# Seven products per tile summed by PSUM in two banks, and six more such tiles, in a spectral mixer with a squared-ReLU layer pair

## The chip, the cores and the metric

One core of one Trainium2 chip runs the whole program. The metric is the device time of one execution in microseconds (us). Before the change it is 845.22 us, the median of three runs (844.39 to 845.75). The engines are called PE (matrix products; PEld is its loading of weights), DVE or VectorE, ACT or ScalarE, POOL or GpSimd, and SP, which issues most transfers.

## What is computed

Eight sequences of 3008 rows and 256 columns go through a mixer in the frequency domain, and the 24064 rows that come out go through two layers:

```python
X = np.fft.rfft(x, axis=1)                       # x: (8, 3008, 256)
Yr = Xr @ w_r - Xi @ w_i + b_r
Yi = Xr @ w_i + Xi @ w_r + b_i
Y  = shrink(Yr, 0.01) + 1j * shrink(Yi, 0.01)    # sign(v) * max(|v| - 0.01, 0)
y  = np.fft.irfft(Y, n=3008, axis=1).reshape(24064, 256)

h = y @ w_in                                     # (24064, 2048)
g = s * np.maximum(h, 0) ** 2 + b
out = g @ w_out                                  # (24064, 256), float32
```

`s` and `b` are single numbers, so `out` is `s * (r*r @ w_out)` plus a row that is the same everywhere (`bias_bc` in the kernel: `b` times the column sums of `w_out`).

## The kernel before, in words

**Tiles.** The rows are cut into 48 tiles of mostly 512 rows (T0 to T47; a few have 480 or 384). T0 to T11 belong to the first two sequences, which the code calls batches. Batches 2 to 7 begin at T12, T17, T23, T29, T35 and T41. For each tile PE makes the first layer in 16 slots: in a slot, the two `psh` matmuls of 512 columns give 128 of the 2048 features (`first_mm`, L847). After every second slot ScalarE rectifies two such blocks (L867: `rt <- psh`), and ScalarE (L877) or VectorE (L880) squares them into `gt`, as 16-bit numbers with the features in partitions. A running account of each engine's load (`work`, `act_first`) chooses which of the two. The second layer of tile T runs one tile later, spread over the 16 slots of T + 1's first layer. Into the same slots go the units of the Fourier stages of other batches (`plan`): the `psf` matmuls, the `ring`, `xf`, `u`, `v` and `yt` operations.

**The plain second layer** (`second_mms`, L918): four groups of 16 matmuls of 256 columns, two groups to a PSUM bank of the pool `psa`; then one VectorE operation on each bank (L941) multiplies by `s`, adds the bias row and gives the output rows, which SP stores. That is 64 matmuls of 256 columns.

**The second layer by seven products** (`seven_mms`, L979). The squares of a tile are seen as two by two blocks a11, a12, a21, a22 (half of the rows; even or odd feature block), and so are the weights w11, w12, w21, w22 (even or odd feature block; half of the output columns). Sums of the weights are made once (`make_t`, L369: T0 to T3). Sums of the squares are made for each tile in two parts, q = 0 and 1 (`s_op`, L961), in place except for the first:

- S1: s1 = a21 + a22
- S3: a21 becomes a11 - a21
- S2: a11 becomes a11 - s1
- S4: a12 becomes a12 + the new a11. This one is an adding DMA that POOL issues (L969), the other three are VectorE's (L976).

The seven products, each of 16 matmuls of 128 columns (two groups of 128 rows, eight feature blocks), are in the numbers that the changed code uses: P1 = a11 w11, P2 = a12 w21, P3 = a12' w22, P4 = a22 T3, P5 = s1 T0, P6 = a11' T1, P7 = a21' T2, where a dash marks a block after its sum. The output blocks are P1 + P2 (top left), P1 + P6 + P5 + P3 (top right), P1 + P6 + P7 + P4 (bottom left) and P1 + P6 + P7 + P5 (bottom right), with all signs in the sums.

Before the change the products come in the order P1, P2, P4, P5, P6, P7, P3 (in the code `left[0]` to `left[6]`), each in its own half of a bank, four banks to a tile from a pool of two. `leave` (L1016) sums them on VectorE in SBUF, in a tile `zz`, in four groups: after P1 and P2 (two adds and one operation with `b_21`, L1026), after P4 (one), after P5 and P6 (one, and one of 512 columns for both halves of `zz`), after P7 and P3 (three), then four stores. A bank is taken again by the next pair of products but one: P5 and P6 wait for the adds of P1 and P2.

Of the 48 tiles 22 are made so (`seven`, L1063): T4 to T7, the two before the start of batches 2 to 7 where they have 480 or 512 rows (10, 11, 15, 16, 21, 22, 27, 33, 34, 39), the second tile of batches 3 to 7 (18, 24, 30, 36, 42), and from T41 on all such but the last two (41, 42, 43, 45).

**Order.** A scheduler lays the program out before it runs: each engine has a fixed order of instructions, near to the order of the code, though an instruction that would wait may be placed behind others. An engine carries out its list in order, so a waiting instruction holds all behind it.

Of the kernel before, what the change touches and what calls it, by code (L numbers as in the profile page):

```python
# [10 lines left out]
F32 = mybir.dt.float32  # L11
ALU = mybir.AluOpType
# [84 lines left out]
def kernel(  # L97
# [48 lines left out]
    apool = ctx.enter_context(tc.tile_pool(name="psa", bufs=2, space=bass.MemoryType.PSUM))  # L146
# [66 lines left out]

    def other_bank():
        return apool.tile([P, 512], F32, name="psa", tag="psa")
# [146 lines left out]
    b_21 = cpool.tile([P, P], F32, name="b_21")  # L362
# [6 lines left out]
    def make_t(i):  # L369

        if not T_s:
            nc.vector.tensor_tensor(
                out=b_21, in0=bias_bc[:, P:D], in1=bias_bc[:, 0:P], op=ALU.subtract
            )
            T_s.append(x2pool.tile([P, 4, MC // 2, P], F16, name="T_s", tag="x2"))
# [584 lines left out]

    def s_op(ti, n, q):  # L961
# [6 lines left out]
        if n == 4:  # L968
            nc.gpsimd.dma_start(out=a12, in_=a11, accum_op=ALU.add)  # L969
            return  # L970
# [3 lines left out]
            2: (a11, a11, s1, ALU.subtract),  # L974
        }[n]
# [3 lines left out]
    def seven_mms(ti):  # L979

        tl = tiles[ti]
        size = sub_size(tl)
        hold = {}
        left = [(0, 0), (0, 1), (1, 1), None, (0, 0), (1, 0), (0, 1)]
        firsts = (0, 2, 3, 5)
        T = T_s[0]
        right = [w_block(0, 0), w_block(1, 0), T[:, 3], T[:, 0], T[:, 1], T[:, 2], w_block(1, 1)]

        def mm(n, j, c):

# [16 lines left out]
        def add(out, of, other):  # L1007
            nc.vector.scalar_tensor_tensor(  # L1008
                out=out, in0=of, scalar=s_bc[0:size], in1=other, op0=ALU.mult, op1=ALU.add
# [3 lines left out]
        def wide(t):  # L1013
            return t[0:size, 0:P].unsqueeze(1).to_broadcast([size, 2, P])

        def leave(group):  # L1016
            if group == 0:
                hold["z"] = zpool.tile([P, 2, 2, P], F32, name="zz", tag="zz")
            if group in (0, 3):
                hold["o", group] = opool.tile([P, 2, D], F32, name="ost", tag="ost")  # L1020
            z = hold["z"][0:size]
            top = hold["o", 0][0:size]
            if group == 0:
                add(z[:, 0], hold[0], wide(bias_bc))
# [3 lines left out]
            elif group == 1:  # L1028
                add(z[:, 0], hold[2], z[:, 0])
            elif group == 2:  # L1030
                add(z[:, 1], hold[3], z[:, 1])
                two = hold[4].rearrange("p j e -> p (j e)").unsqueeze(1).to_broadcast([size, 2, D])
                zs = z.rearrange("p h j e -> p h (j e)")
                add(zs, two, zs)
                work("dve", 0.27)
            else:
                for h in range(2):
                    add(hold["o", 3][0:size, :, h * P : (h + 1) * P], hold[5], z[:, h])
                add(top[:, :, P:D], hold[6], z[:, 1])
                for i in range(2):  # L1040
# [124 lines left out]
```

## Time and profile before

| | us |
|---|---|
| median of three runs | 845.22 (844.39 to 845.75) |
| profiled execution: its time | 843.5 |
| profiled execution: its span, first to last instruction | 841.7 |

The granted clock of TensorE is 0.999 over the span. The costliest groups of instructions, with the mean of one:

| line, engine | operation | count | busy us | mean ns |
|---|---|---|---|---|
| L175 PE | `psh <- yt, w_in`, 512 columns (and 480) | 1344 | 396.6 | 378 |
| L175 PE | `psa <- w_out_t, gt`, 256 and 128 columns | 2432 | 305.9 | 252 |
| L175 PE | `psa <- T_s, gt`, 128 columns | 992 | 83.4 | 219 |
| L867 ACT | rectify, `rt <- psh`, 1024 columns | 384 | 387.0 | 1009 |
| L880 DVE | square, `gt <- rt` | 238 | 285.2 | 1203 |
| L877 ACT | square, `gt <- rt` | 146 | 151.7 | 1039 |
| L969 POOL | adding DMA of S4 (issue) | 44 | 39.7 | 902 |
| L976 DVE | each of S1, S2, S3, 1024 columns | 40 | 27.5 | 687 |
| L941 DVE | output of a plain bank, 512 columns | 41 | 30.7 | 748 |
| L1008 DVE | one add of the seven products, `ost`, 256 columns | 76 | 34.5 | 479 |

A matmul's duration in the profile includes its way through the array; the next one starts long before it ends. So how fast PE goes is read from one start to the next, not from the mean of one. The share of idle time of an engine matters only where another engine waits for it.

### The profile page before, as it was taken

What the parts mean: (1) busy time and instruction counts of PE and PEld (TensorE: products, weight loads), DVE (VectorE), ACT (ScalarE), POOL (GpSimd) and SP (SyncE); (2) the same over time, 40 slices, a digit from 0 to 9 for tenths busy, and PEclk for the clock granted to TensorE, in tenths of its full rate; (3) what the DMA queues carried; (4) which work ended last, traced back from release to release, by engine and by line L of the source; (5) the groups of instructions that cost most, each with busy time, mean ns of one, the idle gap of its engine ahead of it and who ended that gap; (6) DMA issues with size and microseconds to landing.
All of it is one profiled execution on the core that took longest, in us unless ns stands there. A gap on an engine that the chain in (4) does not pass through costs nothing.

```text
span 841.7 us, 19681 instructions
## 1 busy us (share of the span) xinstructions
PE 823.0 (98%) x7710; PEld 599.3 (71%) x7710; DVE 718.2 (85%) x1120; ACT 722.1 (86%) x959; POOL 87.7 (10%) x116
## 2 busy tenths in 40 slices
PE   8999999999999999999999999999999999999997
PEld 7857767777677767776677666777667767767765
DVE  5988989998898888888888888788889888879885
ACT  5998988998899988988899888889879898788882
POOL 4550001110010001100010000100001000001000
PEclk9999999999999999999999999999999999999999
DMA  8954587356873478436773458614565253513322
GB/s 199 180 152 102 124 195 193 63 104 151 202 177 66 107 173 215 105 90 143 188 184 70 96 137 206 168 53 108 131 175 142 51 109 99 144 45 76 71 64 62
DMA packets 116959, 107.70 MB, mean 128 GB/s; under 512 B 12806, under 2 KB 100874, under 8 KB 115522
## 3 DMA queue, kind: packets, MB, share of 16 engines
q1 hardware_dynamic: 102498, 80.55, 33.7%
q0 software_dynamic: 14368, 25.89, 19.4%
q8 instruction: 60, 0.98, 0.5%
q14 instruction: 33, 0.27, 0.1%
HBM read 53.52 MB, written 46.66 MB: 119 GB/s over the span
## 4 chain that ended last, share of the span: by engine, by line
PE 70%; DVE 11%; ACT 8%; DMA 6%; issue 3%; SPq 1%; POOL 0%; DVEq 0%; ACTq 0%; POOLq 0%
PE psh L175 29%; PE psa L175 25%; PE psf L175 15%; ACT rt L867 3%; DVE gt L880 2%; DVE gt L976 2%; ACT gt L877 2%; DMA vd<-v 1%; DMA ring<-ring 1%; DMA x<-in_x_dram 1%; DVE ring L699 1%; DMA vs<-vd 1%; PE psm L175 1%; DMA gt<-gt 1%; DVE s L976 1%
## 5 line engine op out<-in xcount | busy, mean ns | idle before, releaser
L867 ACT ACTIVATE rt<-psh 128x1024 f32<-128x1024 f32 (+2 forms) x384 | 387.0, 1009 | 66.5 <-PE psh L175 64.3
L175 PEld LDWEIGHTS <-gt 128*128 128x128 f16 (+1 forms) x3728 | 305.1, 101 | 167.7 <-DMA gt<-gt 1.2
L175 PE MATMUL psh<-yt,w_in 128*128 128x512 f16 (+1 forms) x1344 | 396.6, 378 | 0.1
L880 DVE TENSOR_TENSOR gt<-rt 128x1024 f16<-128x1024 f32 (+2 forms) x238 | 285.2, 1203 | 61.1 <-ACT rt L867 59.7
L175 PE MATMUL psa<-w_out_t,gt 128*128 128x256 f16 (+3 forms) x2432 | 305.9, 252 | 1.0 <-DMA gt<-gt 1.0
L877 ACT ACTIVATE gt<-rt 128x1024 f16<-128x1024 f32 (+2 forms) x146 | 151.7, 1039 | 3.5
L175 PEld LDWEIGHTS <-w_in 128*128 128x128 f16 x1536 | 136.2, 98 | 25.3 <-issue 2.6
L175 PE MATMUL psa<-T_s,gt 128*128 128x128 f16 (+1 forms) x992 | 83.4, 219 | 0.0
L969 POOL DMA_DIRECT2D gt<-gt x44 | 39.7, 902 | 379.7 <-DVE s L976 200.3
L699 DVE TENSOR_TENSOR ring<-psf,s 128x512 f16<-128x512 f32 x84 | 57.5, 685 | 3.5 <-PE psf L175 2.7
L187 ACT CAST u<-psf 96x512 f16<-96x512 f32 x91 | 52.6, 580 | 9.1 <-PE psf L175 8.9
L187 ACT CAST v<-psf 128x512 f16<-128x512 f32 x82 | 47.5, 582 | 11.1 <-PE psf L175 11.1
L175 PEld LDWEIGHTS <-xf 128*128 128x128 f16 x504 | 46.5, 98 | 8.7 <-DVE xf L672 1.9
L175 PE MATMUL psh<-tail,w_in 128*128 128x512 f16 (+1 forms) x192 | 52.1, 353 | 0.0
L175 PE MATMUL psf<-W_g,xf 128*128 128x256 f16 x336 | 50.4, 272 | 1.0 <-ACT xf L187 1.0
L234 POOL DMA_DIRECT2D x<-in_x_dram x36 | 19.2, 538 | 265.2 <-PE psf L175 264.1
L187 ACT CAST yt<-psf 128x470 f16<-128x470 f32 (+2 forms) x84 | 43.3, 534 | 4.1 <-PE psf L175 2.9
L1008 DVE SCALAR_TENSOR_TENSOR ost<-psa,s_bc,zz 128x256 f32<-128x256 f32 (+1 forms) x84 | 38.1, 479 | 7.2 <-PE psa L175 6.5
L941 DVE SCALAR_TENSOR_TENSOR ost<-psa,s_bc,bias_bc 128x512 f32<-128x512 f32 (+2 forms) x49 | 35.6, 726 | 6.9 <-PE psa L175 5.0
L175 PE MATMUL psf<-x,A_t 94*96 94x512 f16 x102 | 38.9, 381 | 2.0 <-ACT v L187 0.8
L175 PE MATMUL psf<-C_t,vs 96*128 96x94 f16 (+1 forms) x484 | 37.9, 205 | 0.8 <-DMA vs<-vd 0.8
L187 ACT CAST xf<-psf 128x512 f16<-128x512 f32 x62 | 36.2, 584 | 2.1 <-PE psf L175 1.9
(118 smaller groups left out, 810.7 us busy)
## 6 DMA issues: line engine op xcount, KB each, us to landing
out_dram<-ost SPq DMA_DIRECT2D x152, 128.0 KB
ud<-u SPq DMA_DIRECT2D x56, 192.0 KB
us<-ud SPq DMA_DIRECT2D x28, 384.0 KB
vd<-v SPq DMA_DIRECT2D x42, 256.0 KB
vs<-vd SPq DMA_DIRECT2D x14, 768.0 KB
x<-in_x_dram POOLq DMA_DIRECT2D x28, 376.0 KB, 6.1
gt<-gt POOLq DMA_DIRECT2D x40, 256.0 KB, 4.4
ring<-ring SPq DMA_DIRECT2D x280, 32.0 KB
```

The lines of the kernel that those rows point to most:

```text
L175: return nc.tensor.matmul(out, lhs, rhs, **how)
L187: return None, nc.scalar.copy(out=dst, in_=src)
L234: nc.gpsimd.dma_start(out=t[0:N1, i * w : (i + 1) * w], in_=xv[:, c * XCH * D + i * w : c * XCH * D + (i + 1) * w],)
L699: nc.vector.tensor_tensor(out=ring[0][:, i % 4], in0=ps, in1=hold[i // 2][:, i % 2].unsqueeze(1).to_broadcast([P, 2, D]), op=ALU.add,)
L867: nc.scalar.activation(out=rt[:, :, 0:w], in_=ps[:, :, 0:w], func=AF.Relu)
L877: nc.scalar.activation(out=gt, in_=rr, func=AF.Square)
L880: last_square[0] = nc.vector.tensor_tensor(out=gt, in0=rr, in1=rr, op=ALU.mult)
L941: nc.vector.scalar_tensor_tensor(out=ost[0:size, 0:k], in0=ps[0:size, 0:k], scalar=s_bc[0:size], in1=bias_bc[0:size].unsqueeze(1).to_broad ...
L969: nc.gpsimd.dma_start(out=a12, in_=a11, accum_op=ALU.add)
L976: nc.vector.tensor_tensor(out=out, in0=a, in1=b, op=op)
L1008: nc.vector.scalar_tensor_tensor(out=out, in0=of, scalar=s_bc[0:size], in1=other, op0=ALU.mult, op1=ALU.add)
```

## The change

The order of the products becomes P1, P2, P6, P7, P5, P4, P3, and PSUM does a part of the sums: P6, P5 and P3 are added by PE to what P1 left in one bank (x), P4 to what P7 left in the other (y, which P1's partner P2 used before). VectorE reads a bank between two products of its chain, seven reads to a tile, each right after the product that completes what it reads; the operation with `b_21` and the one of 512 columns are no longer there. Tiles of the last batch use a third bank (w) for P4 and P3 and nine reads.

Six more tiles are made by seven products, the third before the start of each of batches 2 to 7 (T9, T14, T20, T26, T32, T38): 28 in all. In these alone S4 is a VectorE sum. The sums S1 and S3 of part 0 move one slot later (three in the last batch), behind the slot's second-layer matmuls. The two banks of the pool `psa` get a tag each, so that the code says which comes next.

```diff
--- before.py
+++ after.py
@@ -143,7 +143,7 @@
 
     cpool = ctx.enter_context(tc.tile_pool(name="consts", bufs=1))
     bigpool = ctx.enter_context(tc.tile_pool(name="big", bufs=1))
-    apool = ctx.enter_context(tc.tile_pool(name="psa", bufs=2, space=bass.MemoryType.PSUM))
+    apool = ctx.enter_context(tc.tile_pool(name="psa", bufs=1, space=bass.MemoryType.PSUM))
     fpool = ctx.enter_context(tc.tile_pool(name="psf", bufs=2, space=bass.MemoryType.PSUM))
     dpool = ctx.enter_context(tc.tile_pool(name="dram", bufs=2, space=bass.MemoryType.DRAM))
     xpool = ctx.enter_context(tc.tile_pool(name="xp", bufs=3))
@@ -211,8 +211,11 @@
     def sum_bank(ti):
         return any_bank() if ti >= mark[B - 1] // MC else other_bank()
 
+    side = [0]
+
     def other_bank():
-        return apool.tile([P, 512], F32, name="psa", tag="psa")
+        side[0] = 1 - side[0]
+        return apool.tile([P, 512], F32, name="psa", tag=f"psa{side[0]}")
 
 
     XCH = 8
@@ -359,7 +362,6 @@
 
 
     w_sum = small[:, 2:4]
-    b_21 = cpool.tile([P, P], F32, name="b_21")
     T_s = []
     last_square = [None]
 
@@ -369,9 +371,6 @@
     def make_t(i):
 
         if not T_s:
-            nc.vector.tensor_tensor(
-                out=b_21, in0=bias_bc[:, P:D], in1=bias_bc[:, 0:P], op=ALU.subtract
-            )
             T_s.append(x2pool.tile([P, 4, MC // 2, P], F16, name="T_s", tag="x2"))
         t = T_s[0]
         a, b, op = (
@@ -958,6 +957,9 @@
         size = 2 * sub_size(tiles[ti])
         return gts[(ti, q)][:, i, k, :, 0:size]
 
+    def third_last(ti):
+        return any(ti == mark[b] // MC - 3 for b in range(2, B))
+
     def s_op(ti, n, q):
 
         size = 2 * sub_size(tiles[ti])
@@ -965,13 +967,14 @@
             sums[(ti, q)] = spool.tile([P, 4, 2 * P], F16, name="s1", tag="s1")
         s1 = sums[(ti, q)][:, :, 0:size]
         a11, a12, a21, a22 = (part(ti, q, i, k) for i in range(2) for k in range(2))
-        if n == 4:
+        if n == 4 and not third_last(ti):
             nc.gpsimd.dma_start(out=a12, in_=a11, accum_op=ALU.add)
             return
         out, a, b, op = {
             1: (s1, a21, a22, ALU.add),
             3: (a21, a11, a21, ALU.subtract),
             2: (a11, a11, s1, ALU.subtract),
+            4: (a12, a12, a11, ALU.add),
         }[n]
         nc.vector.tensor_tensor(out=out, in0=a, in1=b, op=op)
         work("dve", 0.07 + size / 480.0)
@@ -980,84 +983,99 @@
 
         tl = tiles[ti]
         size = sub_size(tl)
+        alone = ti >= mark[B - 1] // MC
+        C = MC // 2
+        T = T_s[0]
+
+
+        of = {
+            1: ((0, 0), w_block(0, 0), "x"), 2: ((0, 1), w_block(1, 0), "y"),
+            4: ((1, 1), T[:, 3], "w" if alone else "y"), 6: ((0, 0), T[:, 1], "x"),
+            7: ((1, 0), T[:, 2], "y"), 5: (None, T[:, 0], "x"),
+            3: ((0, 1), w_block(1, 1), "w" if alone else "x"),
+        }
+        clears = (1, 2, 4, 7, 3) if alone else (1, 2, 7)
         hold = {}
-        left = [(0, 0), (0, 1), (1, 1), None, (0, 0), (1, 0), (0, 1)]
-        firsts = (0, 2, 3, 5)
-        T = T_s[0]
-        right = [w_block(0, 0), w_block(1, 0), T[:, 3], T[:, 0], T[:, 1], T[:, 2], w_block(1, 1)]
 
         def mm(n, j, c):
 
-            if n in firsts and j == 0 and c == 0:
-                hold["ps"] = sum_bank(ti).rearrange("p (n j e) -> p n j e", n=2, j=2)
-            if j == 0 and c == 0:
-                hold[n] = hold["ps"][0:size, 0 if n in firsts else 1]
+            left, right, to = of[n]
+            if to not in hold:
+                hold[to] = sum_bank(ti).rearrange("p (n j e) -> p n j e", n=2, j=2)[0:size, 0]
+                if to == "y" and not alone:
+                    side[0] = 1 - side[0]
             q, g = divmod(c, 4)
             at = slice(j * size, (j + 1) * size)
-            if left[n] is None:
+            if left is None:
                 lhs = sums[(ti, q)][:, g, at]
             else:
-                lhs = gts[(ti, q)][:, left[n][0], left[n][1], g, at]
+                lhs = gts[(ti, q)][:, left[0], left[1], g, at]
             matmul(
-                hold[n][:, j], lhs, right[n][:, c],
-                start=(n in firsts and j == 0 and c == 0), stop=(c == MC // 2 - 1),
+                hold[to][:, j], lhs, right[:, c],
+                start=(n in clears and j == 0 and c == 0), stop=(c == C - 1),
                 skip_group_check=True,
             )
 
-        def add(out, of, other):
+        def add(out, bank, other):
             nc.vector.scalar_tensor_tensor(
-                out=out, in0=of, scalar=s_bc[0:size], in1=other, op0=ALU.mult, op1=ALU.add
+                out=out, in0=hold[bank], scalar=s_bc[0:size], in1=other, op0=ALU.mult, op1=ALU.add
             )
             work("dve", 0.4)
 
-        def wide(t):
-            return t[0:size, 0:P].unsqueeze(1).to_broadcast([size, 2, P])
-
-        def leave(group):
-            if group == 0:
+        def leave(n):
+
+            if n == 1:
                 hold["z"] = zpool.tile([P, 2, 2, P], F32, name="zz", tag="zz")
-            if group in (0, 3):
-                hold["o", group] = opool.tile([P, 2, D], F32, name="ost", tag="ost")
+            if n in (2, 7):
+                hold["o", n] = opool.tile([P, 2, D], F32, name="ost", tag="ost")
             z = hold["z"][0:size]
-            top = hold["o", 0][0:size]
-            if group == 0:
-                add(z[:, 0], hold[0], wide(bias_bc))
-                add(top[:, :, 0:P], hold[1], z[:, 0])
-                nc.vector.tensor_tensor(out=z[:, 1], in0=z[:, 0], in1=wide(b_21), op=ALU.add)
-                work("dve", 0.34)
...
-        C = MC // 2
-        alone = ti >= mark[B - 1] // MC
+            bias = [
+                bias_bc[0:size, h * P : (h + 1) * P].unsqueeze(1).to_broadcast([size, 2, P])
+                for h in range(2)
+            ]
+            top, bot = (hold["o", k][0:size] if ("o", k) in hold else None for k in (2, 7))
+            if n == 1:
+                add(z[:, 0], "x", bias[0])
+            elif n == 2:
+                add(top[:, :, 0:P], "y", z[:, 0])
+            elif n == 4 and alone:
+                add(z[:, 1], "w", bias[0])
+            elif n == 6:
+                add(z[:, 1], "x", z[:, 1] if alone else bias[0])
+            elif n == 7:
+                add(z[:, 0], "y", bias[1])
+            elif n == 5:
+                add(bot[:, :, P:D], "x", z[:, 0])
+            elif n == 3:
+                add(top[:, :, P:D], "w" if alone else "x", z[:, 1] if alone else bias[1])
+                for j in range(2):
+                    store(tl, j, top[:, j, :])
+            if n == (7 if alone else 4):
+                add(bot[:, :, 0:P], "y", z[:, 1])
+            if n == 5 and alone:
+                add(z[:, 1], "x", bias[1])
+            if n == (5 if alone else 4):
+                for j in range(2):
+                    store(tl, 2 + j, bot[:, j, :])
+
+        turns = [1, 2, 4, 6, 7, 5, 3] if alone else [1, 2, 6, 7, 5, 4, 3]
         early = 3 if alone else 2
         order = [
-            (n, j, c) for h in range(2) for n in range(early) for j in range(2)
+            (n, j, c) for h in range(2) for n in turns[:early] for j in range(2)
             for c in range(4 * h, 4 * h + 4)
         ]
-        order += [(n, j, c) for n in range(early, 6) for j in range(2) for c in range(C)]
-        order += [(6, j, c) for h in range(2) for j in range(2) for c in range(4 * h, 4 * h + 4)]
+        order += [
+            (n, j, c) for n in turns[early:] for h in range(2) for j in range(2)
+            for c in range(4 * h, 4 * h + 4)
+        ]
         slots = [[] for _ in range(MC)]
         for at, what in enumerate(order):
             slots[at // 7].append(lambda w=what: mm(*w))
+            if what[1:] == (1, C - 1):
+                slots[at // 7].append(lambda n=what[0]: leave(n))
         for at, n, q in ((2, 2, 0), (2, 1, 1), (2, 4, 0), (3, 3, 1), (4, 2, 1), (5, 4, 1)):
             at += alone and at > 3
             slots[at].append(lambda n=n, q=q: s_op(ti, n, q))
-        for at, group in ((4 + alone, 0), (6, 1), (11, 2), (15, 3)):
-            slots[at].append(lambda group=group: leave(group))
         return slots
 
     def seven(ti):
@@ -1065,7 +1083,7 @@
             return False
         firsts = [mark[b] // MC for b in range(2, B)]
         return (
-            ti >= firsts[-1] or 4 <= ti < 8 or any(m - 2 <= ti < m for m in firsts)
+            ti >= firsts[-1] or 4 <= ti < 8 or any(m - 3 <= ti < m for m in firsts)
             or any(ti == m + 1 for m in firsts[1:])
         )
 
@@ -1127,10 +1145,12 @@
                 for u in plan.pop(ti * MC + mc, []):
                     u()
                 first_mm(ti, mc)
-                if mc in (10, 11) and seven(ti):
-                    s_op(ti, 1 if mc == 10 else 3, 0)
             for u in nxt[mc]:
                 u()
+            if ti < ti_n and seven(ti):
+                at = 13 if ti > mark[B - 1] // MC else 11
+                if mc in (at, at + 1):
+                    s_op(ti, 1 if mc == at else 3, 0)
     assert not plan
 
 
```

More of the change, by code (lines that the diff above doesn't have):

```diff
@@ L1016, in leave @@
-        def leave(group):
-            if group == 0:
+        def leave(n):
+            if n == 1:
                 hold["z"] = zpool.tile([P, 2, 2, P], F32, name="zz", tag="zz")
-            if group in (0, 3):
-                hold["o", group] = opool.tile([P, 2, D], F32, name="ost", tag="ost")
+            if n in (2, 7):
+                hold["o", n] = opool.tile([P, 2, D], F32, name="ost", tag="ost")
             z = hold["z"][0:size]
-            top = hold["o", 0][0:size]
-            if group == 0:
-                add(z[:, 0], hold[0], wide(bias_bc))
-                add(top[:, :, 0:P], hold[1], z[:, 0])
-                nc.vector.tensor_tensor(out=z[:, 1], in0=z[:, 0], in1=wide(b_21), op=ALU.add)
-                work("dve", 0.34)
[L1028 to L1040, printed above, removed]
-                    for j in range(2):
-                        store(tl, 2 * (1 - i) + j, hold["o", 3 * (1 - i)][:, j, :])
```

## Prediction

> Names: T21 is tile 21; its second layer runs while PE does the first layer of tile 22, slot by slot (16 slots, two psh matmuls each). P1 to P7 are the seven products, sixteen matmuls of 128 columns each; z1, z2, z6 and so on are the VectorE adds that read a bank after the product of that number. S1, S2, S3 and S4 are the sums of squared activations, each made in two parts (part 0, part 1).
>
> **What bounds the kernel now.** First the busy time of each engine, on the page:
>
> ```profile
> PE 823.0 (98%) x7710; PEld 599.3 (71%) x7710; DVE 718.2 (85%) x1120; ACT 722.1 (86%) x959; POOL 87.7 (10%) x116
> ```
>
> PE is the bound, if its 98% is work and not modelled ends. So next who PE waits for (us in total, times, longest):
>
> ```profile
> PE psa L175 <- DVE ost L1008: 2.3, 5, 1.0
> PE psm L175 <- DMA x<-in_x_dram: 2.3, 5, 0.8
> PE psf L175 <- DVE ring L699: 1.8, 5, 0.5
> PE psa L175 <- DMA gt<-gt: 1.0, 1, 1.0
> ```
>
> All lines of that answer add to 12.8 us. Then the pace, from the chain of waits in the window 423 to 433 (start us, us, what), where PE goes from T20's plain second layer to T21's products:
>
> ```profile
> 422.97 0.43 PE psh L175 x2
> 423.40 0.44 PE psa L175 x4
> 423.84 0.43 PE psh L175 x2
> 424.27 0.39 PE psa L175 x7
> 424.66 0.21 PE psf L175 x5
> 424.87 0.43 PE psh L175 x2
> ```
>
> Four plain matmuls of 256 columns take 0.44 us (109 ns each), seven of 128 columns 0.39 (55.6 ns), two of psh 0.43: streaming, with nothing lost between. The reader is to see two things: PE time falls only with columns, and any new wait in PE's order is paid in full.
>
> So the decisive view is VectorE's timeline just where the seven products begin, T21's from 423.68 on, with the two ScalarE rows that its squares wait for (start us, us, operation):
>
> ```profile
> 423.88 0.75 DVE L941 SCALAR_TENSOR_TENSOR ost<-psa,s_bc,bias_bc 128x512 f32<-128x512 f32 x1
> 424.55 1.22 DVE L880 TENSOR_TENSOR gt<-rt 128x1024 f16<-128x1024 f32 x1
> 425.69 0.68 DVE L976 TENSOR_TENSOR gt<-gt,s 128x1024 f16<-128x1024 f16 x1
> 426.29 0.68 DVE L976 TENSOR_TENSOR s<-gt 128x1024 f16<-128x1024 f16 x1
> 426.89 1.22 DVE L880 TENSOR_TENSOR gt<-rt 128x1024 f16<-128x1024 f32 x1
> ...
> 429.19 0.68 DVE L976 TENSOR_TENSOR gt<-gt,s 128x1024 f16<-128x1024 f16 x1
> 429.79 0.48 DVE L1008 SCALAR_TENSOR_TENSOR zz<-psa,s_bc,bias_bc 128x256 f32<-128x256 f32 x1
> 430.30 0.49 DVE L1008 SCALAR_TENSOR_TENSOR ost<-psa,s_bc,zz 128x256 f32<-128x256 f32 x1
> ```
>
> ```profile
> 423.49 1.02 ACT L867 ACTIVATE rt<-psh 128x1024 f32<-128x1024 f32 x1
> 425.41 1.03 ACT L867 ACTIVATE rt<-psh 128x1024 f32<-128x1024 f32 x1
> ```
>
> VectorE runs without a gap here. From start to start a square takes 1.14 us, an S sum 0.60, a following independent add 0.40 (two of them at 442.04 and 442.43, 0.39). The adds of P1 and P2 come only at 429.79, though P1 and P2 were done by 428.6: VectorE is over a microsecond late, and PE pays little, because the bank that these adds free is wanted 16 matmuls later.
>
> **The change, part by part.**
>
> PE columns. Each of the six new tiles trades 64 matmuls of 109 ns (6.98 us) for 112 of 55.6 ns (6.23): 0.75 us, 4.5 us for six. The weight loads double in number against columns but ran hidden in the row of seven above. The Trainium skill, "TensorE: Matmul & The Clock Gate", section "Back-to-back issue gap", speaks against it: a sustained stream of weight loads and 128-column matmuls is said to take about 81 ns each. By it 112 of them would be 9.07 us, 2.1 more than the plain tile, and six tiles an estimated 12.6 us slower. The row of this trace says 55.6 ns, in the same stream, and decides.
>
> Old waits removed. In eight tiles the product that takes s as its weights (the fifth in the old order) starts late against the pace, because it waits for the first bank: by the starts of PE's matmuls 0.39, 0.74, 0.31, 0.19, 0.43, 0.19, 1.16 and 0.44 us, together 3.9. One wait of 0.3 for a ring row behind these adds (T7) goes too. Gain 4.2 us.
>
> New waits. This is the part that I expect to decide. P6 now adds into P1's bank and follows P1 and P2. It may not start until z1 has read that bank, and P1's last matmul is only eight matmuls and one slot earlier. Its second half also needs S2 part 1, which VectorE makes behind z1. Both stand behind squares and sums in VectorE's order. I lay the built order of the new program over the measured starts, tile kind by tile kind, from slot 0:
>
> T21's kind (second before a batch; six tiles). The last add (0.48, for 0.75 before) is done by 0.6; the first square waits for the rectifier (424.51, so 0.83) and, at 0.87 as now, ends at 2.01; S2 part 0 to 2.61; the next square waits for its rectifier (426.44: 2.76) to 3.90; S1 part 1 to 4.50; z1 4.50 to 4.98, and PE goes 0.06 later (as at 135.81 + 0.48 to 136.35). PE is at P6 after four slots of 0.43 + 0.39 + 0.21 and 0.43 + 0.22, that is 4.77: wait 0.28. Then S3 (4.90), z2 (5.50) and S2 part 1 (5.90 to 6.58); PE wants it at 5.96 + 0.28: wait 0.40. Sum 0.68.
>
> The new tiles (third before a batch: 9, 14, 20, 26, 32, 38). In the same way T20 from 408.25: the last add to 0.7, square 1.85, S2 2.45, S1 3.05, square 4.20, S4 part 0 (now VectorE's) 4.80, z1 to 5.28, PE at P6 at 4.80: wait 0.54; second half 0.31. Sum 0.85, which eats the tile's 0.75.
>
> The last before a batch (11, 16, 22, 34), T22 from 439.76: the rectifier at 1.1, squares to 2.24 and 4.58, two xf sums, z1 to 5.46, PE at 4.60: 0.92, of which 0.24 is there today as a wait for xf: 0.68.
>
> The second of a batch (18, 24, 30, 36), T30 from 574.99: P6 waits 0.40; the ring row behind it then makes PE wait 0.48 in place of 0.62: net 0.26.
>
> Tiles 4 to 7: 0.8, 1.1, 0.5 and 0.65, sum 3.05. The four of the last batch (41, 42, 43, 45) have three banks and 16 matmuls between; z1 is ready at 5.4 against 5.69: nothing.
>
> Together 6 x 0.68 + 6 x 0.85 + 4 x 0.68 + 4 x 0.26 + 3.05 = 16.0 us. Bounds: 0, if VectorE is one square ahead of this everywhere, and 16.0 + 24 x 0.40 = 25.6, if each of the five operations before z1 takes its full duration and not the start-to-start time, which is 0.08 less. I take 16.0, the nearest to the rows. The skill's "VectorE: DVE Perf Modes", section "The DRAIN you can't avoid", says that the next operation doesn't start until the pipe has emptied. By that rule the upper sum would hold and the kernel lose some 17 us; the rows show starts 0.08 before the end of the one before, so it doesn't hold here.
>
> The other edits. VectorE gets 48 more S sums (0.69: 33 us), 12 plain adds of 0.75 less (9 us), and by 24 x 7 + 4 x 9 adds of 0.48 for 22 times seven of 0.48, one of 0.75 and one of 0.42, 1.7 less: 22 us more, 740 in all, 87%. It is hidden under PE except where counted above; with that cover gone it would be 22 us. The sums S1 and S3 part 0 move from slots 10 and 11 to 11 and 12, or 13 and 14, behind the slot's second-layer matmuls; they are wanted from slot 6 of the next tile on, so nothing, and 0.6 each if VectorE were that late. The stores keep their number; two now leave after P4 and two after P3, so SP, whose ring transfers stand behind stores waiting for L1008 (90.8 us in 13 waits), is held for a shorter time: nothing either way. POOL's 44 adding DMAs stay as they are, since only new tiles use VectorE; the one for which PE waits 1.2 us (T27's second part, at 541.36) is issued up to 0.5 later: 0 to +0.5, taken as 0. The subtraction for b_21 goes, once.
>
> Sum: -4.5 - 4.2 + 16.0 = **+7.3 us**. The profiled execution has a span of 841.7 and a time of 843.5, 1.7 under the median of the runs shown; the difference is put on the median: 845.2 + 7.3 = 852.
>
> **Rivals.**
>
> A, the adds are in time. If VectorE stands a square ahead at P6, the new waits shrink to a third (5 us) and the columns win: -4.5 - 4.2 + 5 = -3.7, 841; with none 836.5. For it: VectorE idles 15%, and in T20's slots 2 to 8 it has gaps of 0.72, 0.94 and 0.46 us. Against: the new sums fill exactly those gaps. It decides once the mean new wait is under 0.36 us (8.7 over 24 tiles).
>
> B, even. New waits near 8.7 us cancel both gains: 845. It needs half of what the rows give.
>
> C, the vector engines become the bound in the new tiles. T20's 15.4 us hold 12.4 of VectorE and 11.8 of ScalarE; six S sums and seven adds for two add 5.1 net, 29.3 of 2 x 14.7 available. If rectifiers then come late, psh stalls as well, by my estimate another 1.3 us in each of six tiles: 860. Against it: the squares are shared out anew, and in the built order VectorE's share is 13.0.
>
> D, the change does not chain as it says. The built order has 576 rows more on PE (six times 96) and a wait on VectorE before P6: it does.
>
> **How the numbers follow.** Forecast 0.54, its own range 847 to 857 (new waits 11 to 21 us). C 0.10, B 0.10, A 0.26. The range 842 to 859 takes in B and a part of A and leaves out A's best and C's worst. Beyond 0.2% (1.7 us) is what a measurement of this kernel tells from none; faster A, 0.26; same B, 0.10; slower the forecast and C, 0.64.
>
> **What would show it.** Right: PE waits for DVE zz at P6 in about 20 tiles, 0.3 to 0.9 us each, and for gt (S2) at its second half; PE busy time or matmul pace unchanged; the old wait at T_s,s gone. Wrong: fewer than ten such waits (A), or ScalarE's waits for psh turned into PE's waits for ScalarE (C). The sum fails if VectorE reaches z1 half a microsecond sooner than by the old starts, or if 128-column matmuls stop streaming at 55.6 ns.

## The result, and the profile after

| | us | ratio to before, 95% interval |
|---|---|---|
| before, beside it | 844.81 (843.89 to 845.75, 4 runs) | |
| after | 854.75 (852.85 to 856.65, 4 runs) | 1.0119 [1.0097, 1.0141] |

The change makes the kernel slower by 1.2%. The profiled execution took 854.7, with a span of 852.9, 11.2 us over that of before; its granted clock is again 0.999.

Engines, from the page of the kernel after:

```profile
PE 823.8 (97%) x7998; PEld 598.8 (70%) x7998; DVE 728.1 (85%) x1151; ACT 726.2 (85%) x969; POOL 87.3 (10%) x116
```

PE issues 288 matmuls more (six tiles, 112 for 64) and VectorE is busy 9.9 us longer. PE is still the busiest engine. What PE waits for (us in total, times, longest):

```profile
PE psa L175 <- DVE zz L1020: 7.6, 19, 0.8
PE psf L175 <- DVE v L189: 3.9, 5, 0.8
PE psm L175 <- DMA x<-in_x_dram: 2.6, 6, 0.8
PE psf L175 <- DVE xf L671: 1.8, 4, 0.6
...
PE psa L175 <- DVE gt L979: 1.1, 5, 0.2
```

The first and the last line are P6's: 19 waits for z1, five for S2. The second was not there before: `v` came from ScalarE, at 0.8 us of waits. Now T21's products, as before: VectorE (start us, us, operation)

```profile
430.14 1.23 DVE L879 TENSOR_TENSOR gt<-rt 128x1024 f16<-128x1024 f32 x1 [0.79 <-ACT rt L866]
431.28 0.69 DVE L979 TENSOR_TENSOR gt<-gt,s 128x1024 f16<-128x1024 f16 x1
431.88 1.22 DVE L879 TENSOR_TENSOR gt<-rt 128x1024 f16<-128x1024 f32 x1
433.02 0.69 DVE L979 TENSOR_TENSOR s<-gt 128x1024 f16<-128x1024 f16 x1
433.62 0.48 DVE L1020 SCALAR_TENSOR_TENSOR zz<-psa,s_bc,bias_bc 128x256 f32<-128x256 f32 x1
434.01 0.68 DVE L979 TENSOR_TENSOR gt<-gt 128x1024 f16<-128x1024 f16 x1
434.61 0.48 DVE L1020 SCALAR_TENSOR_TENSOR ost<-psa,s_bc,zz 128x256 f32<-128x256 f32 x1
435.01 0.68 DVE L979 TENSOR_TENSOR gt<-gt,s 128x1024 f16<-128x1024 f16 x1
```

PE at the same place:

```profile
433.23 0.39 PE L175 MATMUL psa<-w_out_t,gt 128*128 128x128 f16 x4
434.15 0.33 PE L175 MATMUL psa<-T_s,gt 128*128 128x128 f16 x3 [0.54 <-DVE zz L1020]
...
435.75 0.28 PE L175 MATMUL psa<-T_s,gt 128*128 128x128 f16 x2 [0.22 <-DVE gt L979]
```

and ScalarE:

```profile
427.66 1.06 ACT L876 ACTIVATE gt<-rt 128x1024 f16<-128x1024 f32 x1
...
429.08 1.02 ACT L866 ACTIVATE rt<-psh 128x1024 f32<-128x1024 f32 x1
```

P6 starts at 434.15, 0.05 after z1's end (433.62 + 0.48). By the pace it was due at 433.45: 0.70 lost. Its second half waits again, for S2, which ends at 435.69. The view of waits counts 0.54 and 0.22, since it counts from the modelled end of the matmul before. So below, *excess* is what PE loses from start to start: the time by which a matmul starts later than the one before plus 55.5, 109 or 216 ns (128, 256, 512 columns).

The span of a tile is here the stretch in which PE makes the tile's second layer, beside the first layer of the next tile.

| excess, us, in the spans of | before | after | chain only | six only | sums out | own bank | own bank, 22 |
|---|---|---|---|---|---|---|---|
| new tiles (T9, T14, T20, ...) | 0.7 | 4.0 | 0.7 | 5.6 | 3.7 | 2.9 | 0.7 |
| second before a batch (T10, T21, ...) | 4.9 | 8.0 | 9.7 | 8.4 | 3.7 | 4.7 | 4.6 |
| last before a batch (T11, T22, ...) | 1.6 | 4.1 | 4.1 | 1.6 | 2.8 | 5.9 | 5.2 |
| second of a batch (T18, T30, ...) | 6.1 | 5.5 | 5.5 | 6.2 | 3.7 | 3.9 | 3.8 |
| T4 to T7 | 3.1 | 4.8 | 4.8 | 3.2 | 3.5 | 4.7 | 4.7 |
| the tile before a new one (T8, T13, T19, ...) | 1.2 | 5.6 | 2.5 | 4.3 | 5.6 | 5.6 | 0.9 |
| last batch | 0.2 | 0.9 | 0.9 | 0.5 | 0.9 | 0.9 | 0.9 |
| rest | 3.8 | 4.7 | 3.1 | 3.2 | 3.1 | 4.1 | 2.9 |
| all | 21.5 | 37.5 | 31.2 | 32.9 | 26.9 | 32.6 | 23.8 |

(The columns on the right are experiments told below.) After less before is +15.9 (before rounding); less the 4.5 us of columns that fell away this is +11.4, and the span grew by 11.2. That the same sum also meets the spans of the runs on the right within 0.7 us (sums out: 5.4 - 4.5 = +0.9, span +0.9) shows, to within that 0.7, that the six tiles' columns are worth the 4.5, and that all else is waits.

The term that the prediction didn't have is in the tile before a new one. T19's second layer, VectorE:

```profile
411.45 1.23 DVE L879 TENSOR_TENSOR gt<-rt 128x1024 f16<-128x1024 f32 x1
412.60 0.68 DVE L189 CAST v<-psf 128x512 f16<-128x512 f32 x1
```

and PE:

```profile
411.94 0.60 PE L175 MATMUL psa<-w_out_t,gt 128*128 128x256 f16 x4
413.33 0.38 PE L175 MATMUL psf<-x,A_t 94*96 94x512 f16 x1 [0.79 <-DVE v L189]
```

The cast of `v` empties a `psf` bank. Before, ScalarE made the cast at this place, and PE went on without a loss:

```profile
407.36 0.58 ACT L187 CAST v<-psf 128x512 f16<-128x512 f32 x1 [0.20 <-PE psf L175]
```

```profile
408.03 0.38 PE L175 MATMUL psf<-x,A_t 94*96 94x512 f16 x1
```

Of the 84 such casts ScalarE made 82 before and 72 after. In T8, T19, T25 and T31 the running account gives the cast to VectorE, where it stands behind a square, and PE waits for the bank: 0.95 us of excess each. A fifth such wait, 0.89 us in T13, is for a cast that stands behind eight copies of `ring`.

### The profile page after: what moved, and what is told of

It is laid out like the page before. It is cut to its first block, busy times and chain, and to the rows that moved or that the text cites. A ratio compares the mean times of both kernels' runs of the same rounds, so it can differ in the third digit from the quotient of the medians.

```text
span 852.9 us, 20352 instructions
## 1 busy us (share of the span) xinstructions
PE 823.8 (97%) x7998; PEld 598.8 (70%) x7998; DVE 728.1 (85%) x1151; ACT 726.2 (85%) x969; POOL 87.3 (10%) x116
## 5 line engine op out<-in xcount | busy, mean ns | idle before, releaser
L175 PEld LDWEIGHTS <-gt 128*128 128x128 f16 (+1 forms) x3920 | 308.5, 100 | 175.7 <-issue 12.5
L879 DVE TENSOR_TENSOR gt<-rt 128x1024 f16<-128x1024 f32 (+2 forms) x241 | 288.3, 1198 | 66.6 <-ACT rt L866 65.4
L175 PE MATMUL psa<-w_out_t,gt 128*128 128x256 f16 (+3 forms) x2384 | 278.4, 244 | 1.0 <-DMA gt<-gt 0.6
L175 PE MATMUL psa<-T_s,gt 128*128 128x128 f16 (+1 forms) x1248 | 110.2, 219 | 9.2 <-DVE zz L1020 7.6
L187 ACT CAST yt<-psf 128x470 f16<-128x470 f32 (+2 forms) x95 | 49.4, 523 | 5.6 <-PE psf L175 3.4
L187 ACT CAST xf<-psf 128x512 f16<-128x512 f32 x75 | 44.0, 587 | 7.8 <-PE psf L175 7.7
L187 ACT CAST v<-psf 128x512 f16<-128x512 f32 x72 | 41.7, 580 | 10.4 <-PE psf L175 10.4
L979 DVE TENSOR_TENSOR gt<-gt 128x1024 f16<-128x1024 f16 (+1 forms) x68 | 46.4, 682 | 0.3
L175 PEld LDWEIGHTS <-s 128*128 128x128 f16 (+1 forms) x448 | 31.2, 100 | 15.0
L1020 DVE SCALAR_TENSOR_TENSOR zz<-psa,s_bc,bias_bc 128x256 f32<-128x256 f32 (+1 forms) x80 | 38.3, 478 | 2.7 <-PE psa L175 2.5
```

The costliest lines, as they stand in the source:

```text
L175: return nc.tensor.matmul(out, lhs, rhs, **how)
L187: return None, nc.scalar.copy(out=dst, in_=src)
L879: last_square[0] = nc.vector.tensor_tensor(out=gt, in0=rr, in1=rr, op=ALU.mult)
L979: nc.vector.tensor_tensor(out=out, in0=a, in1=b, op=op)
L1020: nc.vector.scalar_tensor_tensor(out=out, in0=hold[bank], scalar=s_bc[0:size], in1=other, op0=ALU.mult, op1=ALU.add)
```

## The experiments

Each is measured beside the kernel before, on the same chip. Runs are medians of 5 to 12.

| | us | before | ratio, 95% interval |
|---|---|---|---|
| chain only | 853.20 | 843.91 | 1.0106 [1.0077, 1.0134] |
| six only | 849.48 | 843.91 | 1.0061 [1.0039, 1.0084] |
| v on ScalarE | 853.09 | 843.91 | 1.0104 [1.0081, 1.0127] |
| no z1 | 852.54 | 843.91 | 1.0095 [1.0072, 1.0119] |
| P4 third | 850.17 | 843.88 | 1.0072 [1.0051, 1.0092] |
| P4 third, v on ScalarE | 848.59 | 843.88 | 1.0055 [1.0035, 1.0076] |
| sums back | 853.97 | 843.88 | 1.0115 [1.0093, 1.0136] |
| S1 later | 857.43 | 843.88 | 1.0158 [1.0134, 1.0182] |
| own bank | 851.91 | 844.95 | 1.0082 [1.0061, 1.0103] |
| own bank, v on ScalarE | 848.82 | 844.95 | 1.0050 [1.0028, 1.0071] |
| own bank, 22 tiles | 846.84 | 844.95 | 1.0031 [1.0017, 1.0044] |
| sums out | 844.77 | 843.50 | 1.0016 [1.0000, 1.0033] |

**Chain only**: the kernel after with the 22 old tiles.

```diff
-            ti >= firsts[-1] or 4 <= ti < 8 or any(m - 3 <= ti < m for m in firsts)
+            ti >= firsts[-1] or 4 <= ti < 8 or any(m - 2 <= ti < m for m in firsts)
```

> The chains in PSUM alone, on the 22 tiles of before. Theory (P6 has to wait for z1 in its bank; the six new tiles give 4.5 us of PE and lose as much again by v casts that move to VectorE in the tiles before them): the chain's own part is about +7 us, 849 to 854; PE waits for zz at P6 about 0.3 to 0.9 us in most of the 18 tiles that have two banks; no wait of 0.95 us for a v cast in the tiles before T9, T14, T20, T26, T32. Rival (VectorE's load as a whole is what costs, and it comes with the six tiles): the chain takes work off VectorE, so 844 to 846.

The theory held: 9.3 us slower. P6's first matmul loses 7.3 us in 15 tiles and its second half 3.2; the 3.9 us at the fifth product are gone. Not all of the rest is the chain's: PE's wait for a transfer of `vs` is 1.9 us longer than before (2.9 for 1.0 of excess), and the kernel after has none. VectorE has here no more sums than before and is busy 709.8 us, 8.4 less than before: it isn't its load as a whole.

**Six only**: the kernel before with the six tiles, and S4 there on VectorE.

```diff
-        if n == 4:
+        if n == 4 and not third_last(ti):
...
+            4: (a12, a12, a11, ALU.add),
...
-            ti >= firsts[-1] or 4 <= ti < 8 or any(m - 2 <= ti < m for m in firsts)
+            ti >= firsts[-1] or 4 <= ti < 8 or any(m - 3 <= ti < m for m in firsts)
```

> The six new tiles alone, with S4 on VectorE, summed on VectorE as before. Theory: -4.5 us of PE columns, +4.4 by v casts on VectorE (0.95 each in five tiles before the new ones, by the trace of after), +1.8 by the old wait at the fifth product (0.3 in six tiles): 846.5, 843 to 849. Rival (VectorE's load): nearly all of the loss is here, 852 to 857.

A little over the expectation's upper end. PE's waits have the reason on their first line:

```profile
PE psa L175 <- DVE ost L1012: 8.3, 12, 1.0
```

These are the old waits of the fifth product for the first bank: 11.0 us of excess in 15 places, where 8 lost 3.9 before. With +3.1 in the tile before they eat the columns and 6 us more. But that 3.1 isn't the wait that the expectation had there: 2.0 of it is for a transfer of `ring` in T8's span and 0.9 for a `v` cast in T13. In T19, T25 and T31 VectorE makes a `v` cast here too, and PE doesn't wait for it. So each half of the change costs by itself, and both through a bank that VectorE reads too late. Together they cost less than their sum (1.0106 and 1.0061 against 1.0119), since the chain takes away the wait that the six tiles make longer.

**v on ScalarE**: the cast of `v` always there.

```diff
-            evac(v[:, h : h + 2, :], ps, 512)
+            nc.scalar.copy(out=v[:, h : h + 2, :], in_=ps)
+            work("act", over["act"] + 512 / 1200.0)
```

> The changed kernel with all v casts of the later batches on ScalarE, as nearly all were before. Theory: the five waits of 0.95 us for psf in the tiles before the new ones go, and ScalarE takes eight more casts of 0.58 us in its idle time: 854.75 - 4.4 = 850.3, 849 to 852. Rival (VectorE is late there anyway, the cast is only what stands in front): 853 to 855.

It gave 0.15% (1.0119 to 1.0104, the intervals lie one on the other), some 1.3 us, not 4.4. The excess in the tile before a new one fell from 5.6 to 2.2, somewhat less than expected (in T13 VectorE now has a `u` cast in the same place, and PE loses the same 0.88), but in the new tile P6's wait grew (T20: 0.39 to 0.66 us), and its spans together from 4.0 to 5.7. There z1 comes later: a wait taken away in one tile turned up in part in the next. The spans second before a batch grew by 1.8 as well, nearly all of it one wait in T15 for a transfer of `vs`, which the kernel after doesn't have.

**No z1**: the first add left out, so that P1 is missing in the top left block.

```diff
-            if n == 1:
-                add(z[:, 0], "x", bias[0])
-            elif n == 2:
-                add(top[:, :, 0:P], "y", z[:, 0])
+            if n == 2:
+                add(top[:, :, 0:P], "y", bias[0])
```

> The changed kernel without z1 in the 28 tiles: the add that reads P1 is left out, so P1 is missing in the top left block of the output, and P6 need not wait for a read of its bank. Theory: the waits at P6's first matmul (11.9 us by starts, 7.6 of them named as waits for zz) shrink to what S2 leaves, under 4: 845 to 848. Rival (VectorE's load): one add of 0.48 us less in 28 tiles of VectorE's 728, of which perhaps a tenth shows: 853 to 855.

A miss, and the most useful one. The waits at P6's first matmul are gone, but PE now waits eight matmuls on:

```profile
PE psa L175 <- DVE gt L979: 6.0, 14, 0.7
```

This is S2 of part 1, 10.3 us of excess at P6's second half (in the kernel after 11.3 at its first matmul and 3.1 at the second half). So the bank read in the middle of the chain isn't the cause alone: P6 as third product wants two things early, and VectorE has neither ready.

**Sums back**: S1 and S3 of part 0 in slots 10 and 11 again.

```diff
+                if mc in (10, 11) and seven(ti):
+                    s_op(ti, 1 if mc == 10 else 3, 0)
...
-            if ti < ti_n and seven(ti):
-                at = 13 if ti > mark[B - 1] // MC else 11
-                if mc in (at, at + 1):
-                    s_op(ti, 1 if mc == at else 3, 0)
```

> The changed kernel with S1 and S3 of part 0 back in slots 10 and 11, ahead of the slot's second-layer matmuls, as before the change. Theory: the move cost nothing, 853 to 856. Rival (the move put these sums into the squares' way at the end of a tile and so made VectorE late at the start of the next): 848 to 851.

As the theory said: nothing (the intervals of this and the kernel after lie one on the other). But not nothing everywhere: the tile before a new one fell from 5.6 to 1.8, the new tiles rose from 4.0 to 7.3. At the end of T19 the cast of `v` is on VectorE here too, but ahead of the square, and in T20 z1 is later:

```profile
412.30 0.69 DVE L189 CAST v<-psf 128x512 f16<-128x512 f32 x1
413.02 1.23 DVE L879 TENSOR_TENSOR gt<-rt 128x1024 f16<-128x1024 f32 x1
...
418.90 0.48 DVE L1020 SCALAR_TENSOR_TENSOR zz<-psa,s_bc,bias_bc 128x256 f32<-128x256 f32 x1
```

```profile
413.23 0.38 PE L175 MATMUL psf<-x,A_t 94*96 94x512 f16 x1
...
419.43 0.33 PE L175 MATMUL psa<-T_s,gt 128*128 128x128 f16 x3 [1.00 <-DVE zz L1020]
```

So a cast on VectorE isn't enough for the wait in the tile before. The later place of S1 and S3, the only difference between the two kernels, brings the square in front of it; and what PE doesn't lose there it loses at P6 in the next tile.

**S1 later**: S1, S3 and S2 of part 1 all behind z1.

```diff
-        for at, n, q in ((2, 2, 0), (2, 1, 1), (2, 4, 0), (3, 3, 1), (4, 2, 1), (5, 4, 1)):
+        early_sums = ((2, 2, 0), (2, 1, 1), (2, 4, 0), (3, 3, 1), (4, 2, 1), (5, 4, 1))
+        late_sums = ((2, 2, 0), (2, 4, 0), (4, 1, 1), (4, 3, 1), (4, 2, 1), (5, 4, 1))
+        for at, n, q in early_sums if alone else late_sums:
```

> The changed kernel with S1 and S3 of part 1 behind z1 (slot 4), so that z1 comes some 0.6 us sooner in VectorE's order and S2 of part 1 no sooner. Theory (P6 needs z1 for its first half and S2 of part 1 for its second, and both are late): the wait at P6's first matmul falls by half and the one at its second half grows as much, 853 to 856. Rival (z1 alone is the wait): 846 to 850.

Slower still by 0.4%, and over what was expected; the intervals of this and the kernel after just meet. P6's first matmul gained only 1.5 (11.3 to 9.8), since the squares ahead of z1 stay, and what was put off is late behind it: 3.6 at the second half for 3.1, and 1.6 at P7 for 0.3. This order at least doesn't help where the queue as a whole is late.

**P4 third** gives P6 another product's distance: P4 goes into the other half of P2's bank, z2 behind z4, with one add more. In a second kernel `v` is on ScalarE too.

```diff
-            4: ((1, 1), T[:, 3], "w" if alone else "y"), 6: ((0, 0), T[:, 1], "x"),
+            4: ((1, 1), T[:, 3], "w"), 6: ((0, 0), T[:, 1], "x"),
...
+                    hold["w"] = bank[0:size, 1]
...
-        turns = [1, 2, 4, 6, 7, 5, 3] if alone else [1, 2, 6, 7, 5, 4, 3]
-        early = 3 if alone else 2
+        turns = [1, 2, 4, 6, 7, 5, 3]
+        early = 3
```

> The changed kernel with P4 as the third product, in the other half of P2's bank, and P6 fourth; P6, P5 and P3 still chain onto P1, P7 no longer meets P4; z2 is made behind the add that reads P4, and there is one add more per tile. Theory (what costs is that P6 comes third, so that PE meets z1 and both parts of S2 before VectorE has made them): waits at P6 nearly go, 0.3 us per tile at most stay somewhere, the 4.4 us of waits behind v casts stay: 841 to 847. Rival (VectorE is so late at the start of a tile that whatever comes third or fourth waits as long; one add more makes it worse): 851 to 856.

> The same with all v casts of the later batches on ScalarE. Theory: the waits behind v casts in the tiles before the new ones go as well, 2 to 4 us under the kernel with P4 third: 838 to 844. Rival (as with the chain as it was, where half came back as waits at the next tile's products): 1 to 2 us under it.

Between theory and rival. P6 is cured (three places, 1.6 us), but P3 now follows P5 in one bank. T20's end, VectorE:

```profile
427.44 1.21 DVE L879 TENSOR_TENSOR gt<-rt 128x1024 f16<-128x1024 f32 x1
428.57 0.68 DVE L979 TENSOR_TENSOR s<-gt 128x1024 f16<-128x1024 f16 x1
429.17 0.48 DVE L1022 SCALAR_TENSOR_TENSOR ost<-psa,s_bc,zz 128x256 f32<-128x256 f32 x1
```

and PE:

```profile
427.35 0.44 PE L175 MATMUL psa<-T_s,s 128*128 128x128 f16 x5
...
429.70 1.05 PE L175 MATMUL psa<-w_out_t,gt 128*128 128x128 f16 x16 [0.61 <-DVE ost L1022]
```

P5 ends near 427.8. Its reader stands behind a square and T21's S1 and ends at 429.65; all sixteen matmuls of P3 wait until 429.70. Chain x holds P1, P6, P5 and P3 and wants a product of another bank between each two; P2, P7 and P4 are just three, so P6 third or two neighbours is the choice. `v` on ScalarE brought 1.6 us, the rival's size, though the intervals of the two kernels overlap.

**Own bank**: P4 third, and P3 no longer added in x but in a bank of its own (nine adds), with `v` where the account puts it, on ScalarE, and on the 22 old tiles alone.

```diff
-            3: ((0, 1), w_block(1, 1), "w" if alone else "x"),
+            3: ((0, 1), w_block(1, 1), "w" if alone else "v"),
...
-            if n == 5 and alone:
+            if n == 5:
                 add(z[:, 1], "x", bias[1])
```

> P4 third in the other half of P2's bank as before, and P3 no longer added into P5's bank but into a bank of its own (the one that P2, P4 and P7 used), with one more VectorE add: nine to a tile in place of eight. Theory: the waits left with P4 third (850.17) are waits of P3, directly behind P5 in one bank, for VectorE's read of P5, 16 places of 0.4 to 0.85 us, about 10 us. P3 in another bank needs only the reads behind P7, sixteen matmuls earlier, so most of them go and nothing else is late by as much: 840 to 845, level with or under the kernel before (843.9). Rival: VectorE stays late whatever the banks, and the next tile's P1 and P2, or the plain tile's second bank, wait for the reads of P5 and P3 in place of P3: 848 to 852.

> The same with the v casts on ScalarE throughout. Theory: with the queue at the seven products out of PE's way, the casts' 3.5 us in the tiles before the new ones come out whole: 837 to 842, 3 to 4 us under the same kernel without. Rival: they are given back in the tiles behind, as they were twice before: 1 to 2 us under it.

> P4 third and P3 in its own bank on the 22 old tiles alone, v where the planner puts it. Theory: the old waits at the fifth product (3.9 us) are gone and nothing takes their place: 840 to 843, under the kernel before by 1 to 4 us; the six tiles more are then worth no more than 0 to 3 us. Rival: the waits move on as in the runs before: 845 to 849.

The rival held in the first: no better than with P3 in the chain. P3 waits less (2.9 us, 6 times), but T22's P1, which takes T21's bank x, waits for the second read of P5. VectorE:

```profile
444.24 1.16 DVE L979 TENSOR_TENSOR gt<-gt 128x1024 f16<-128x1024 f16 x1
445.32 0.47 DVE L1022 SCALAR_TENSOR_TENSOR zz<-psa,s_bc,bias_bc 128x256 f32<-128x256 f32 x1
```

and PE:

```profile
444.56 0.59 PE L175 MATMUL psh<-yt,w_in 128*128 128x512 f16 x2
445.85 0.56 PE L175 MATMUL psa<-w_out_t,gt 128*128 128x128 f16 x7 [0.70 <-DVE zz L1022]
```

6.9 us go so, at the first product in 11 tiles. With `v` on ScalarE the time is 3.1 us less, the size that the theory gave, though from a higher level; the two intervals overlap a little, so the size is not sure. On 22 tiles the chain without P3 costs 0.3% in place of the 1.1% of the chain only. It is the best of the kernels that compute the whole, and still behind the kernel before. The six more tiles cost here 0.5% again (1.0082 against 1.0031).

**Sums out**: the kernel after without S2 and without S3 of part 1, with the account unchanged.

```diff
-        nc.vector.tensor_tensor(out=out, in0=a, in1=b, op=op)
+        if n != 2 and (n, q) != (3, 1):
+            nc.vector.tensor_tensor(out=out, in0=a, in1=b, op=op)
```

> The changed kernel with three of the sums of squares left out in all 28 tiles: S2 in both parts and S3 of part 1 (so P6 uses the plain a11 and P7 the plain a21 in part 1, and those output blocks differ); the planner's account, and with it the share of the squares, stays. This takes 0.6 us of VectorE's queue from before z1 in most tiles, and 1.2 us more from behind it. Theory, that the price of the chain is VectorE's lateness in slots 2 to 6 and nothing of the banks or of PE: the waits at P6 (11.9 us) fall to 2 us or less and, since the queue itself is shorter, do not come back elsewhere: 843 to 847. Rival, that the waits move to the next reader of a bank as in the runs before: 850 to 854.

The blocks that these sums belong to come out different. Some 9 us come back by the ratios (10.3 by the spans), in the range of the theory, and no new wait of that size takes their place: PE's matmuls, the banks and the order of the products are those of the kernel after, and VectorE's queue is shorter (682.3 us busy for 728.1). Not all of it is the queue's, though: P6's second half has no S2 to wait for any more, which takes its 3.1 us away in any case, and 1.7 of the 10.3 is a wait for a transfer of `ring` in T2's span, before any of these tiles. Waits for `xf` fell by 2.2. At P6 less went than expected:

```profile
PE psa L175 <- DVE zz L1021: 4.5, 11, 0.7
```

The second half is free (3.1 to 0), and the excess of T21's kind fell by 4.3 us, but the first matmul still loses 7.5 us in 17 tiles for 11.3 in 22. In T20's kind it isn't the queue's length: VectorE idles 0.54 us until a rectifier ends at 412.20, and behind that come a square, S4 and z1:

```profile
412.23 1.23 DVE L879 TENSOR_TENSOR gt<-rt 128x1024 f16<-128x1024 f32 x1 [0.54 <-ACT rt L866]
413.37 0.68 DVE L980 TENSOR_TENSOR gt<-gt 128x1024 f16<-128x1024 f16 x1
413.98 0.48 DVE L1021 SCALAR_TENSOR_TENSOR zz<-psa,s_bc,bias_bc 128x256 f32<-128x256 f32 x1
```

How much the fixed place of that square alone costs wasn't tried.

## Why the prediction came out

**Columns, -4.5**: right. Seven matmuls of 128 columns still take 0.39 us, also in the new tiles, and the balance of excess and span closes with 4.5. The Trainium skill's figure for such a stream ("TensorE: Matmul & The Clock Gate", "Back-to-back issue gap", 81 ns), which would have made the tiles dearer, doesn't show in any run.

**Old waits, -4.2**: right, as far as they can be told apart; no wait at a weight block `T_s,s` for the first bank is left in the kernel after. The six-only run shows that without the chain these would have grown to 11.0.

**New waits, +16.0**: the mechanism and the places are right, the sum at P6 is 14.4 (11.3 at its first matmul in 22 tiles, 3.1 at its second half in 16 places). The parts are off in both directions:

- T21's kind: forecast 0.28 and 0.40, measured 0.70 and 0.38. The step that failed is that the first square starts "at 0.87 as now". A square just ahead of the slot, now on ScalarE (427.66 above), and a cast of `u` behind it put the rectifier off to 430.10, 1.44 us behind the slot's start in place of 0.83; z1 is later by as much less the time that the next square then need not wait.
- New tiles: forecast 0.85, measured 0.39 in most. z1 ends 5.16 after slot 0, near the 5.28 of the sum, but in most the second half was not held up.
- Last before a batch: forecast 2.7 in all, measured 2.5, but not as the forecast had it. In T22 P6 lost 0.42 and not 0.92, and the wait for `xf` of 0.24, which was to go into P6's, grew to 0.57. In T11 all of the new wait is for `xf`.
- T30: forecast 0.40 at P6, measured 0.30.
- Tiles 4 to 7: forecast 0.8, 1.1, 0.5, 0.65; measured at the first matmul 0.50, 0.93, 0.38 and nothing in T7, where the second half loses 0.57.
- Last batch: forecast nothing, measured 0.7 more than before, 0.52 of it at one P6.

**The other edits, 0**: here a term is missing. VectorE's 22 us were taken to hide under PE "except where counted above", and rival C looked for the harm in the rectifiers of the new tiles. The harm was in the tile before: +4.4 us, nearly all of it at five of the ten `v` casts that the account moved to VectorE. The forecast looked at the products' own tiles and not at the whole program's order. The sums' later slots cost nothing in all, as said (sums back), but not for the reason given, that the sums are wanted later: they put the square in front of the cast and so take 3.8 us in the tile before, and P6 in the new tiles waits about as much less. VectorE's busy time rose by 9.9, not 22: for the ten casts of `v` that it took, the account gave it 13 casts of `xf` and 11 of `yt` less (22 to 9, 23 to 12).

**The sum**: +7.3 forecast, +11.2 in span. In the spans of the other tiles made by seven products, without the last batch, the excess grew by 10.0, where the forecast had 16.0 - 4.2 = 11.8: 1.8 too much. Not foreseen were 4.4 in the tile before, 0.7 at the last batch and 0.9 for a transfer of `ring` while PE makes T3's first layer. That last one may be chance: chain only and six only have no such wait there, but one of 1.5 and 2.0 us in T8's span. Errors in both directions partly cancelled; the direction rested on the right wait, and without any of these surprises the waits at P6 alone would have outweighed both gains.

**The rivals.** A (adds in time) fell at the mean wait: 14.4 over 24 tiles is 0.60, over its 0.36. B fell with it. C fell: PE hardly waits for ScalarE. D holds: the chain is there, and PE waits in it. What the experiments add to the forecast is that z1 isn't the only thing late (no z1), and that moving the read elsewhere moves the wait (P4 third, own bank). The common cause is VectorE's lateness in the first slots of a tile: with three sums fewer there the loss goes from 1.2% to 0.2% (sums out), though a part of that is S2's own wait. Why VectorE is late is shown in part only: it waits for ScalarE's rectifiers too, 65.4 us in 97 waits (59.7 in 79 before), and no run here separates this from the length of its queue.

**Two readings.** At 442.04 and 442.43 the prediction saw two adds; the second is a cast of `xf`. The 0.39 us from the add's start to that of the next operation holds. And it set the rows against the Trainium skill's "VectorE: DVE Perf Modes", section "The DRAIN you can't avoid". That section itself adds that a next operation which is not held starts earlier, so the starts 0.08 before the end of the one before don't speak against it.

The Trainium skill asks, in "PSUM — Partial Sum Buffer", section "PSUM bank collisions raise a hardware error", that PE's writes and VectorE's reads of a bank be kept apart by a wait. The traces show that wait at its price: 0.05 us from the end of a read to PE's next matmul in that bank (434.10 to 434.15), and everything that VectorE is late on top of it. P6 adds onto the very numbers that z1 reads, so it has to wait for that reason as well.

## What to carry to other kernels

Summing in PSUM saves adds, but each sum that is read in the middle of a chain makes the next product wait for the reader: count, for each pair of neighbours in a bank, the matmuls between them against how late the reading engine is at that moment, not against its mean load. When a change adds work that a load account distributes, compare the whole order of every engine, tiles around the change included: here the costliest surprise was a cast in the tile before, and what made it cost was the place of a square in front of it. If waits of one cause reappear wherever the banks are moved, shorten the late queue first; here that was tried only by leaving work out.

## What was not expected of the hardware

The sum at 444.24 in the own-bank kernel took 1.16 us, where the same operation takes 0.68 at 434.01 in the kernel after. At that time POOL was copying:

```profile
443.93 0.94 POOL L800 COPY tail<-yt 128x896 f16<-128x896 f16 x1 [6.95 <-DVE s L979]
```

Of this run's 180 sums four met such a copy, by 0.60 to 0.71 us, and took 1.14 to 1.23; the other 176 took under 0.76. The sum ends 0.53 us after the copy does, and alone it takes 0.68, so it hardly went on meanwhile. The Trainium skill ("SBUF — State Buffer", "Who interferes with whom") states that a VectorE instruction with two inputs in SBUF contends with a GpSimd instruction that reads SBUF; the four fit that. The add behind this sum is the one that T22's P1 waits for, so up to 0.48 (1.16 less 0.68) of its 0.86 us of excess may have come from a copy that no wait names, and so in the other three, whose waits are all in the span of the last tile before a batch. A copy moved out of the way wasn't tried. In the kernels before and after no copy met a sum.
